# Another order of products in the last unit of each GEMM, constant matmuls ahead of the first ones, and an earlier load of the last rows

## The chip, the cores and the metric

The kernel runs on one core of a Trainium2 chip. The metric is the device time of one execution in microseconds; lower is better. The core has TensorE (PE), VectorE (DVE), ScalarE (ACT), GpSimd (POOL) and SyncE (SP), each with its own instruction stream, and 16 DMA engines. SP issues loads and stores, POOL issues transfers that add to what is in the result.

## The reference

The layer adds three things for S = 2048 rows of D = 1024: the input itself, a gated long convolution, and a feed-forward part with F = 3584.

```python
def _A_ref(q, k, v, shift_k, ssm_k, ssm_D):      # q = layernorm(x)
    k_shift = ...                                # 4-tap causal convolution of k by channel
    kv = k_shift * v
    y = irfft(rfft(kv, 2 * S) * rfft(ssm_k, 2 * S))[:S]   # causal convolution of length S
    return q * (y + kv * ssm_D)
def _B_ref(x, w1, w2):                           # x = layernorm(x)
    return silu(x @ w1) @ w2
return x + _A_ref(xn, ...) + _B_ref(xn, w1, w2)
```

Everything is in float32. Only the shapes and types of this decide the time.

## The kernel before, in words

**Products.** Every operand of a GEMM is split into a high and a low float16 part, and a product of two operands takes three matmuls (high by high, high by low, low by high) for each of four steps of 128 in the inner dimension: 12 matmuls of 512 columns. `steps` (L941, matmuls L946 to L948) does it for GEMM1, x @ w1, `steps2` (L1070, matmuls L1074 to L1076) for GEMM2, silu(...) @ w2.

**Units.** Most of GEMM1 is done by the scheme of Strassen and Winograd: a unit makes a block of two by two with seven products P1 to P7 rather than eight. `UNITS` lists 26 of them (12 for the upper half of the rows, sp = 0, then 14 for the lower half, sp = 1); four plain units with eight products stand ahead. GEMM2 begins with plain products, row tile by row tile in two halves of the columns (`TOGETHER` says which row tiles run side by side, so that they share the loaded weights), and ends with eight units of seven products (`tiles2`, L1079).

Within a unit the results are gathered partly in PSUM: P1 opens the bank `one`, ScalarE copies it into the bank `two`, then P2 is added to `one`, and P6, P5 and P3 one after another to `two`, with an eviction by ScalarE after P6 and after P5; P7 opens the bank `c`, and P4 is added to it after VectorE has read it. The order in which TensorE does them, written out in `units` (L982) and `units2` (L1092), is P7, P6, P2, P5, P1 of the next unit, P3, P4. In the last unit there is no next P1, so that P3 follows P5. `evacuate` (L909) and `evacuate2` (L1139) are the other half: what ScalarE and VectorE do with each bank. `evacuate2` scales by `invc2` and sends the four blocks of the unit to the result: three with `G` (L344), an accumulating DMA that POOL issues, and for the last unit the fourth block differently: the rows that are already in the result are loaded (`L`, L334, SP's queue), added by VectorE, and the sum is stored.

**Convolution.** It is done by a DFT as matmuls: a forward stage 1 (L1520 to L1522), products with the filter's spectrum, and an inverse (L1711 to L1713), for groups of channels `g`. They are interleaved with the GEMMs.

**Buffers.** `ff` is a ring of four PSUM banks for the products. `hfs` is a ring of three buffers with two halves each (`hf` in the trace; `vs_r` and `ws_r` are the same ring), `hts` one of two (`ht`). `places` are eight large places for factors; `XPLACE`, `W2PLACE` and `FPLACE` say what lies where and when.

**Order.** Nothing is ordered by hand beyond that. Each of the generators above is a stream, `Order.run` (L177) takes again and again the stream whose next operation can start first by a modelled clock, less a bias given to the stream:

```python
t = max(self.free[s.head.eng], s.at)
if best is None or t - s.bias < best[0]:
    best = t - s.bias, t, s
```

An operation has a modelled cost and a margin after its inputs (`T(mm, ps, [hi, lo], 0.65, m=1.0)` for TensorE). `yield ff.ready` holds a stream until a bank of the ring is free in that order, `yield made["P5"]` until another stream has issued what it names. So every edit of a cost or of a wait moves instructions of all engines elsewhere too.

**Start.** `warm_up` (L1785) issues 22 matmuls of a constant 128 by 128 tile while the first rows are loaded. Then the rows are normalized (L579), transposed by TensorE (L598), split in two by ScalarE (L360) and VectorE (L352), and the first plain unit begins.

Of the kernel before, what the change touches and what calls it, by code (L numbers as in the profile page):

```python
# [11 lines left out]
F32 = mybir.dt.float32  # L12
# [46 lines left out]
W2PLACE = [(2, 7, 6, 3, 4), (0, 1, 5, 2, 7)]  # L59
FPLACE = (6, 3, 4, 0, 1, 5, 2, 7)  # L60
# [240 lines left out]
def h3_ffn_kernel(ctx, tc, x, kp, vs, fs, shift, dskip, w1, w2, cfwd, cinv, out):  # L301
# [607 lines left out]
    def evacuate(i, b, one, c, made, seen):  # L909
# [17 lines left out]
        seen["P5"].set()  # L927
        low, done = yield from places_of(i, b + 1)
# [10 lines left out]
        add(silu(i, low, low, None, done), EB)  # L939

# [126 lines left out]
    TOGETHER = ([range(2)] + [(t,) for t in range(2, NT)],  # L1067
                [(t,) for t in range(NT - 3)] + [range(NT - 3, NT)])

    def steps2(po, hx, wc, first, last, more=False):  # L1070
        for n in range(4):
# [5 lines left out]
            yield T(mm, po, [hx[:, n], wc[:, n]], 3 * 0.2185)  # L1077
# [14 lines left out]
    def units2():  # L1092

        def product2(n, u, o, first=False):
# [4 lines left out]
            yield from steps2(o, hx, wc, first, True, not first)  # L1099
            htok.set()  # L1100
            if u == len(tiles2) - 1:
                wtok.set()

        yield ff.ready
        one = ff.tile([P, W])
        yield from product2("P1", 0, one[0], True)
        for u in range(len(tiles2)):
            made, seen = defaultdict(Token), defaultdict(Token)
            yield ff.ready
            c = ff.tile([P, W])  # L1110
            add(evacuate2(u, one, c, made, seen), EB)
            yield from product2("P7", u, c[0], True)
# [4 lines left out]
            yield from product2("P2", u, one[0])  # L1117
            made["P2"].set()
            yield seen["P6"]
            yield from product2("P5", u, two)  # L1120
            made["P5"].set()
            if u + 1 < len(tiles2):
                yield ff.ready
                one = ff.tile([P, W])
                yield from product2("P1", u + 1, one[0], True)
# [4 lines left out]
            yield from product2("P4", u, c[0])  # L1130
            made["P4"].set()
# [7 lines left out]
    def evacuate2(u, one, c, made, seen):  # L1139
# [3 lines left out]
        def copied(src, tok, to):  # L1143
            yield hfs.ready
            o, otok = hfs.tile([P, W])
# [14 lines left out]
        yield made["P2"]  # L1160
        add(copied(*one, at(u, 0, 0)), EB)
# [4 lines left out]
        seen["P5"].set()  # L1166
# [625 lines left out]
    def load_factors_late():  # L1792
        yield flag["w done"]
        yield from load_factors()
# [59 lines left out]
```

## Time and profile before

| | |
|---|---|
| median of three runs | 1255.85 us |
| the three runs | 1255.65, 1255.85, 1258.87 us |
| the profiled execution | 1258.14 us |
| its span, first to last instruction | 1256.4 us |
| mean granted clock of TensorE | 0.994 |
| TensorE busy | 1232.6 us (98%) |
| VectorE busy | 1117.9 us (89%) |
| ScalarE busy | 790.5 us (63%) |

In the profile, a row of a timeline gives the start in us, the duration, the engine, the line, the operation and its tiles (out <- in), the count, and in brackets how long the engine had been idle before and what ended that. A matmul's duration reaches to the end of its pipeline; matmuls that follow one another start closer than they last. The granted clock is 1.00 at full speed and 0.50 where the chip halves TensorE's clock.

### The profile page before, as it was taken

What the parts mean: (1) busy time and instruction counts of PE and PEld (TensorE: products, weight loads), DVE (VectorE), ACT (ScalarE), POOL (GpSimd) and SP (SyncE); (2) the same over time, 40 slices, a digit from 0 to 9 for tenths busy, and PEclk for the clock granted to TensorE, in tenths of its full rate; (3) what the DMA queues carried; (4) which work ended last, traced back from release to release, by engine and by line L of the source; (5) the groups of instructions that cost most, each with busy time, mean ns of one, the idle gap of its engine ahead of it and who ended that gap; (6) DMA issues with size and microseconds to landing.
All of it is one profiled execution on the core that took longest, in us unless ns stands there. A gap on an engine that the chain in (4) does not pass through costs nothing. (4 is left out here: it accounts for less than half of the span.)

```text
span 1256.4 us, 17146 instructions
## 1 busy us (share of the span) xinstructions
PE 1232.6 (98%) x6034; PEld 597.5 (48%) x6034; DVE 1117.9 (89%) x1359; ACT 790.5 (63%) x1431; POOL 83.5 (7%) x93
## 2 busy tenths in 40 slices
PE   7999999999999999999999999999999999999996
PEld 6554444444444544444444544544544544454452
DVE  7999987997999789998999899799989889988970
ACT  7868888886588878568654643744653545563351
POOL 0000000000000000000000000000120030123132
PEclk8999999999999999999999999999999999999999
DMA  9276989989799899769984655688595497969765
GB/s 367 82 262 239 315 288 303 300 240 227 232 336 270 242 309 313 207 191 297 311 278 125 206 179 132 185 269 231 107 257 153 106 225 217 243 137 161 164 121 80
DMA packets 272662, 279.83 MB, mean 223 GB/s; under 512 B 73792, under 2 KB 192576, under 8 KB 271296
## 3 DMA queue, kind: packets, MB, share of 16 engines
q1 hardware_dynamic: 256848, 262.22, 67.9%
q0 software_dynamic: 15728, 16.52, 9.9%
q8 instruction: 47, 0.77, 0.3%
q14 instruction: 39, 0.32, 0.1%
HBM read 175.66 MB, written 88.34 MB: 210 GB/s over the span
## 5 line engine op out<-in xcount | busy, mean ns | idle before, releaser
L1074 PE MATMUL ff<-x,wo 128*128 128x512 f16 x864 | 327.9, 380 | 3.4 <-ACT hf L360 3.4
L1076 PE MATMUL ff<-x,wo 128*128 128x512 f16 x864 | 328.1, 380 | 0.0
L1075 PE MATMUL ff<-x,wo 128*128 128x512 f16 x864 | 327.9, 380 | 0.1
L946 PE MATMUL ff<-x,wo 128*128 128x512 f16 (+1 forms) x808 | 304.5, 377 | 6.2 <-ACT hf L360 3.0
L948 PE MATMUL ff<-x,wo 128*128 128x512 f16 (+1 forms) x808 | 304.8, 377 | 1.0 <-DVE wo L352 1.0
L947 PE MATMUL ff<-x,wo 128*128 128x512 f16 (+1 forms) x808 | 304.8, 377 | 0.0
L349 DVE TENSOR_TENSOR spec<-spec 128x512 f32<-128x512 f32 (+2 forms) x256 | 261.8, 1053 | 2.0
L1075 PEld LDWEIGHTS <-wo 128*128 128x128 f16 x864 | 84.6, 98 | 104.0 <-issue 4.7
L1076 PEld LDWEIGHTS <-wo 128*128 128x128 f16 x864 | 84.6, 98 | 102.6 <-issue 1.0
L1074 PEld LDWEIGHTS <-wo 128*128 128x128 f16 x864 | 85.5, 99 | 100.1 <-issue 0.6
L948 PEld LDWEIGHTS <-wo 128*128 128x128 f16 x808 | 79.6, 98 | 94.3 <-DVE wo L352 1.5
L947 PEld LDWEIGHTS <-wo 128*128 128x128 f16 x808 | 79.5, 98 | 93.8 <-issue 5.8
L946 PEld LDWEIGHTS <-wo 128*128 128x128 f16 x808 | 81.0, 100 | 90.2 <-ACT wo L360 1.7
L349 DVE TENSOR_TENSOR tmp<-spec 128x2048 f32<-128x2048 f32 (+1 forms) x48 | 92.7, 1933 | 0.9
L352 DVE SCALAR_TENSOR_TENSOR ht<-hf,wsc,ht 128x1024 f16<-128x1024 f32 (+1 forms) x56 | 67.4, 1203 | 7.5 <-ACT ht L360 7.2
L360 ACT ACTIVATE spec<-ps 128x512 f32<-128x512 f32 x92 | 53.2, 592 | 28.7 <-PE ps L1522 28.0
L352 DVE SCALAR_TENSOR_TENSOR wo<-raw,wsc,wo 128x512 f16<-128x512 f32 (+1 forms) x56 | 56.4, 1012 | 11.9 <-ACT wo L360 11.9
L346 POOL DMA_DIRECT2D out<-hf x47 | 45.8, 981 | 303.9 <-ACT hf L360 254.4
L360 ACT ACTIVATE hf<-ff,invc 128x512 f32<-128x512 f32 x32 | 21.9, 684 | 65.7 <-PE ff L1076 47.6
L360 ACT ACTIVATE ht<-hf,wsc 128x1024 f16<-128x1024 f32 (+1 forms) x56 | 60.8, 1085 | 3.4 <-DVE hf L349 2.1
L360 ACT ACTIVATE spec<-spec 128x1024 bf16<-128x1024 f32 x32 | 33.7, 1054 | 46.1 <-DVE spec L349 46.0
L349 DVE TENSOR_TENSOR spec<-tmp 128x512 f32<-128x512 f32 (+1 forms) x80 | 61.3, 792 | 0.7
(188 smaller groups left out, 1779.3 us busy)
## 6 DMA issues: line engine op xcount, KB each, us to landing
wo<-hs SPq DMA_DIRECT2D x160, 256.0 KB, 3.2
hs<-ht SPq DMA_DIRECT2D x80, 256.0 KB, 4.8
raw<-in_w SPq DMA_DIRECT2D x28, 512.0 KB, 5.9
wraw<-in_w SPq DMA_DIRECT2D x24, 512.0 KB, 5.4
w2n<-in_w SPq DMA_DIRECT2D x24, 512.0 KB, 6.1
out<-hf POOLq DMA_DIRECT2D x47, 256.0 KB, 4.5
kin<-in_kp SPq DMA_DIRECT2D x16, 704.0 KB, 5.1
xt<-in_x SPq DMA_DIRECT2D x16, 512.0 KB, 7.3
```

What stands on the lines that cost most here:

```text
L346: return Op("POOL", 1.1, 3.0, lambda: nc.gpsimd.dma_start(o, i, accum_op=ADD), [i], [o], m, 2.3 * n)
L349: return V(lambda: nc.vector.tensor_tensor(o, a, b, op=op), o, [a, b], **k)
L352: return V(lambda: nc.vector.scalar_tensor_tensor(o, a, s, b, op0=op0, op1=op1), o, [a, b] + ([] if isinstance(s, float) else [s]), **k)
L360: nc.scalar.activation(o, i, func, scale=scale, **kw)
L946: nc.tensor.matmul(o, w[:, 0, k], xf[:, :, k, 0], start=first and k == 0, stop=False, **kw)
L947: nc.tensor.matmul(o, w[:, 0, k], xf[:, :, k, 1], start=False, stop=False, **kw)
L948: nc.tensor.matmul(o, w[:, 1, k], xf[:, :, k, 0], start=False, stop=last and k == KH - 1, **kw)
L1074: nc.tensor.matmul(po, hx[:, n, 0, :], wc[:, n, 0, :], start=first and n == 0, stop=False, **kw)
L1075: nc.tensor.matmul(po, hx[:, n, 0, :], wc[:, n, 1, :], start=False, stop=False, **kw)
L1076: nc.tensor.matmul(po, hx[:, n, 1, :], wc[:, n, 0, :], start=False, stop=last and n == 3, **kw)
```

## The change

- In the last unit of each GEMM the order of the products is P6, P7, P5, P2, P3, P4.
- `start` does P1 of a unit and begins its evacuation, which takes the bank `two`, in all units; the bank `c` is taken later, by `seventh`, just before P7.
- In the last unit of GEMM2, the rows of the result for the fourth block are loaded as soon as P6 is evicted, into a half of `hts`; copies to the result may use `hts` as well; P4 is done in two halves of 256 columns, each added and stored by itself.
- `keep_warm` issues matmuls of the constant tile, into a bank of `ff`, until the last transpose of the first rows has been issued: 23 in all, 14 of them between the second group of transposes and the first product.
- The places of some factors are exchanged, the first group of GEMM2's row tiles has three rather than two, a product's modelled cost goes with its columns, and one margin in the forward stage of the convolution is 3.0 in place of 1.0 for the first step of every group but the first.

```diff
-W2PLACE = [(2, 7, 6, 3, 4), (0, 1, 5, 2, 7)]
-FPLACE = (6, 3, 4, 0, 1, 5, 2, 7)
+W2PLACE = [(2, 6, 4, 0, 3), (1, 5, 7, 2, 6)]
+FPLACE = (4, 0, 3, 1, 5, 7, 2, 6)
 
...
         for sp in range(2):
             yield flag["room", sp]
-            yield places[4].ready
-            t, tok = places[4].tile([P, 2, 2 * W], F32)
+            r = places[(4, XPLACE["S3"])[sp]]
+            yield r.ready
+            t, tok = r.tile([P, 2, 2 * W], F32)
...
         yield made["P6"]
         yield a_act(u, two, AF.Copy)
         seen["P6"].set()
-        yield made["P2"]
-        up, both = yield from places_of(i, b)
-        add(silu(i, up[:, 0], *one, both), EB)
+
+        def first():
+            up, both = quads_up[i, b] = yield from places_of(i, b)
+            add(silu(i, up[:, 0], *one, both), EB)
+        if early:
+            yield made["P2"]
+            yield from first()
         yield ws_r.ready
         d, dt = ws_r.tile([P, 4, P])
         yield made["P5"]
         yield a_act(d, two, AF.Copy)
         seen["P5"].set()
+        c = seen["c"]
+        if not early:
+            yield made["P2"]
+            yield from first()
+        up, both = quads_up.pop((i, b))
         low, done = yield from places_of(i, b + 1)
         yield v_tt(low[:, 1], c[0], d, ADD)
...
         todo = [(i, sp) for sp in range(2) for i in UNITS[sp]]
-        yield ff.ready
-        one = ff.tile([P, 4, P])
-        yield from product("P1", *todo[0], one[0], True)
+
+        def start(n):
+            i, sp = todo[n]
+            yield ff.ready
+            one = ff.tile([P, 4, P])
+            yield from product("P1", i, sp, one[0], True)
+            made, seen = defaultdict(Token), defaultdict(Token)
+            add(evacuate(i, 2 * sp, one, made, seen, n + 1 < len(todo)), EB)
+            return one, made, seen
+
+        following = yield from start(0)
         for n, (i, sp) in enumerate(todo):
             if sp == 1:
                 flag["unit", n - len(UNITS[0])].set()
                 flag["room", 1].set()
             if i in PAIRS:
                 add(quad(i, sp), 0.1)
-            made, seen = defaultdict(Token), defaultdict(Token)
-            yield ff.ready
-            c = ff.tile([P, 4, P])
-            add(evacuate(i, 2 * sp, one, c, made, seen), EB)
-            yield from product("P7", i, sp, c[0], True)
+            one, made, seen = following
+
+            def seventh():
+                yield ff.ready
+                seen["c"] = c = ff.tile([P, 4, P])
+                yield from product("P7", i, sp, c[0], True)
+
+            def second():
+                yield from product("P2", i, sp, one[0])
+                made["P2"].set()
+            final = n + 1 == len(todo)
+            if not final:
+                yield from seventh()
             yield seen["P1"]
             two = seen["bank"][0]
             yield from product("P6", i, sp, two)
             made["P6"].set()
-            yield from product("P2", i, sp, one[0])
-            made["P2"].set()
+            yield from seventh() if final else second()
             yield seen["P6"]
             yield from product("P5", i, sp, two)
             made["P5"].set()
+            if final:
+                yield from second()
             if n + 1 < len(todo):
-                yield ff.ready
-                one = ff.tile([P, 4, P])
-                yield from product("P1", *todo[n + 1], one[0], True)
+                following = yield from start(n + 1)
             yield seen["P5"]
             yield from product("P3", i, sp, two)
             made["P3"].set()
             yield seen["P7"]
-            yield from product("P4", i, sp, c[0])
+            yield from product("P4", i, sp, seen["c"][0])
             made["P4"].set()
 
     def load_x():
         yield flag["spilled"]
-        for name in [p[0] for p in PRODUCTS.values()]:
-            r = places[XPLACE[name]]
+        for name in ("S3", "A11", "S2", "A12", "S1", "S4", "A22"):
+            r = places[4 if name == "S3" else XPLACE[name]]
             yield r.ready
...
 
 
-    TOGETHER = ([range(2)] + [(t,) for t in range(2, NT)],
+    TOGETHER = ([range(3)] + [(t,) for t in range(3, NT)],
                 [(t,) for t in range(NT - 3)] + [range(NT - 3, NT)])
...
+            yield T(mm, po, [hx[:, n], wc[:, n]], 3 * 0.2185 * size(po) / W)
...
         for u in range(len(tiles2)):
-            for n in ("P7", "P6", "P2", "P5"):
+            for n in ("P7", "P6", "P2", "P5") if u + 1 < len(tiles2) else ("P6", "P7", "P5", "P2"):
                 yield u, n
...
-        def product2(n, u, o, first=False):
+        def product2(n, u, o, first=False, cols=slice(0, W), end=True):
             yield flag["h2", u, n]
             hx, htok = flag["h2", u, n].what
             yield flag["w2f", n]
             wc, wtok = w2f[n]
-            yield from steps2(o, hx, wc, first, True, not first)
-            htok.set()
-            if u == len(tiles2) - 1:
-                wtok.set()
-
-        yield ff.ready
-        one = ff.tile([P, W])
-        yield from product2("P1", 0, one[0], True)
+            yield from steps2(o[:, cols], hx, wc[:, :, :, cols], first, True, not first)
+            if end:
+                htok.set()
+                if u == len(tiles2) - 1:
+                    wtok.set()
...
-            yield from product2("P4", u, c[0])
-            made["P4"].set()
+            if u + 1 < len(tiles2):
+                yield from product2("P4", u, seen["c"][0])
+                made["P4"].set()
+                continue
+            for q in range(2):
+                yield from product2("P4", u, seen["c"][0], cols=slice(q * W // 2, (q + 1) * W // 2), end=q == 1)
+                made["P4", q].set()
...
-    def evacuate2(u, one, c, made, seen):
+    def evacuate2(u, one, made, seen):
 
         last = u == len(tiles2) - 1
 
         def copied(src, tok, to):
-            yield hfs.ready
-            o, otok = hfs.tile([P, W])
+            yield lambda: hfs.ready() or last and hts.ready()
...
         yield made["P6"]
         yield a_act(a, two, AF.Copy, invc2[:, 0:1])
         seen["P6"].set()
-        yield made["P2"]
-        add(copied(*one, at(u, 0, 0)), EB)
+        if last:
+            yield flag["conv out"]
+            yield hts.ready
+            o, otok = hts.tile([P, W])
+            yield L(o, at(u, 1, 0))
+        if not last:
+            yield made["P2"]
+            add(copied(*one, at(u, 0, 0)), EB)
         yield ws_r.ready
         d, dt = ws_r.tile([P, W])
         yield made["P5"]
         yield a_act(d, two, AF.Copy, invc2[:, 0:1])
         seen["P5"].set()
+        c = seen["c"]
         yield v_stt(d, c[0], invc2[:, 0:1], d, MUL, ADD)
         seen["P7"].set()
+        if last:
+            yield made["P2"]
+            add(copied(*one, at(u, 0, 0)), EB)
         yield G(at(u, 1, 1), d)
         dt.set()
         if last:
-            yield flag["conv out"]
-            yield hfs.ready
-            o, otok = hfs.tile([P, W])
-            yield L(o, at(u, 1, 0))
             yield v_tt(a, a, o, ADD)
             otok.set()
         yield made["P3"]
         add(copied(two, k2, at(u, 0, 1)), EB)
-        yield made["P4"]
-        yield v_stt(a, c[0], invc2[:, 0:1], a, MUL, ADD)
+        if not last:
+            yield made["P4"]
+            yield v_stt(a, c[0], invc2[:, 0:1], a, MUL, ADD)
+            c[1].set()
+            yield G(at(u, 1, 0), a)
+            at_.set()
+            return
+        for q in range(2):
+            yield made["P4", q]
+            cols = slice(q * W // 2, (q + 1) * W // 2)
+            yield v_stt(a[:, cols], c[0][:, cols], invc2[:, 0:1], a[:, cols], MUL, ADD)
+            yield L(at(u, 1, 0)[:, cols], a[:, cols])
         c[1].set()
-        yield L(at(u, 1, 0), a) if last else G(at(u, 1, 0), a)
         at_.set()
...
+                            yield T(mm, ps, [hi, lo], 0.65, m=3.0 if g > 0 and t == TO[0] else 1.0)
                             (made if i else two[c][3]).set()
...
         tok.set()
 
+    def keep_warm():
+
+        pt, tok = ff.tile([P, 4, P])
+        while not flag["turned", "A12", 3]():
+            yield T(lambda: nc.tensor.matmul(pt[:, 0, :], ones, ones, start=True, stop=True), pt[:, 0, :], [], 0.22)
+        tok.set()
...
+    add(keep_warm(), -0.3)
     add(x_rows(), 0.13)
     add(ln_rows(), 0.03)
```

The order of the products in `uses2`, which gives the order of the loads, follows; so does the rest of `units2`, which is changed as `units` is.

More of the change, by code (lines that the diff above doesn't have):

```diff
@@ L907, in places_of, with evacuate @@
         return hf, made
-    def evacuate(i, b, one, c, made, seen):
+    def evacuate(i, b, one, made, seen, early):
         yield ff.ready
@@ L939, in evacuate @@
         add(silu(i, low, low, None, done), EB)
+    quads_up = {}
     def steps(o, w, xf, first, last, more=False):
@@ L1116, in units2 @@
             made["P6"].set()
-            yield from product2("P2", u, one[0])
-            made["P2"].set()
+            yield from seventh() if final else second()
             yield seen["P6"]
@@ L1121, in units2 @@
             made["P5"].set()
+            if final:
+                yield from second()
             if u + 1 < len(tiles2):
-                yield ff.ready
-                one = ff.tile([P, W])
-                yield from product2("P1", u + 1, one[0], True)
+                following = yield from start(u + 1)
             yield seen["P5"]
@@ L1137, in at @@
         return orr[t // T2, t % T2, :, h * W:(h + 1) * W]
-    def evacuate2(u, one, c, made, seen):
+    def evacuate2(u, one, made, seen):
         last = u == len(tiles2) - 1
         def copied(src, tok, to):
-            yield hfs.ready
-            o, otok = hfs.tile([P, W])
+            yield lambda: hfs.ready() or last and hts.ready()
+            o, otok = (hts if last and hts.ready() else hfs).tile([P, W])
             yield a_act(o, src, AF.Copy, invc2[:, 0:1])
```

26 lines of the change are left out of this document (19 added, 7 removed).

## The prediction

> **What bounds the kernel.** I read the page first, then the waits, then the timeline of each place that the waits named, and last the windows around them.
>
> ```profile
> span 1256.4 us, 17146 instructions
> PE 1232.6 (98%) x6034; PEld 597.5 (48%) x6034; DVE 1117.9 (89%) x1359; ACT 790.5 (63%) x1431; POOL 83.5 (7%) x93
> PEclk8999999999999999999999999999999999999999
> ```
>
> TensorE is busy for 98% of the span, so a kernel that does the same products can gain only where TensorE is idle, where it runs at less than full clock, or where something runs after it has ended. VectorE with 89% is the engine that could become late next. The waits of TensorE name the idle places:
>
> ```profile
> PE ff L1074 <- ACT hf L360: 3.4, 2, 2.7
> PE ff L946 <- ACT hf L360: 3.0, 1, 3.0
> ...
> PE ff L946 <- DVE hf L349: 1.8, 1, 1.8
> ```
>
> The columns are microseconds in all, times, and the longest. In the whole of GEMM1's products (L946) TensorE waited once for an eviction by ScalarE, in GEMM2's (L1074) twice; the timeline puts all three into the two last units. The windows add what the idle time costs behind it; the columns that I use are the stretch, its length, PE's busy time and, third from the end, the granted clock:
>
> ```profile
> 11.40:14.80 3.40, 1.08 (x7) 0.56 (x7) 3.23 (x12) 3.16 (x8) 0.00 (x0) 1.00 1.08 406
> 14.80:21.60 6.80, 5.83 (x28) 4.06 (x28) 6.66 (x17) 6.15 (x15) 0.00 (x0) 0.50 1.03 416
> ...
> 588.20:591.60 3.40, 3.40 (x9) 1.19 (x8) 3.37 (x4) 1.88 (x6) 0.00 (x0) 0.50 1.06 323
> ...
> 1240.20:1243.60 3.40, 3.03 (x8) 0.92 (x7) 0.00 (x0) 1.02 (x2) 0.86 (x1) 0.50 0.25 21
> ```
>
> There are three places at half clock: the first products, the last unit of GEMM1, and the last unit of GEMM2. The three edits aim at the same three places, so the working has three terms and a remainder. All are savings against the profiled execution, which took 1258.14 us for its span of 1256.4 (1.74 lie outside the span); the median of the three runs is 1255.85, 2.29 lower.
>
> **First term: the constant matmuls at the start.**
>
> ```profile
> 6.43 1.50 PE L1789 MATMUL ft<-one 128*128 128x128 f32 x12
> ...
> 12.38 0.66 PE L598 MATMUL ft<-ident,xt 128*128 128x128 f32 x4 [0.87 <-DVE x L352]
> 14.48 0.28 PE L946 MATMUL ff<-x,wo 128*128 128x256 f16 x1 [1.45 <-ACT wo L360]
> 16.07 0.40 PE L948 MATMUL ff<-x,wo 128*128 128x256 f16 x1 [0.97 <-DVE wo L352]
> 22.49 0.27 PE L948 MATMUL ff<-x,wo 128*128 128x256 f16 x1
> 22.60 1.47 PE L598 MATMUL ft<-ident,xt 128*128 128x128 f32 x12
> ...
> 20.17 0.81 DVE L579 TENSOR_SCALAR xt<-xt,ag,rstd 128x1024 f32<-128x1024 f32 x1
> 23.87 1.89 DVE L352 SCALAR_TENSOR_TENSOR x<-ft,x 128x512 f16<-128x512 f32 x3 [1.72 <-ACT x L360]
> ```
>
> The loop that warms up now (L1789, 22 instructions, each seen as two such records) gives 12 records in 1.50 us, hence 1.50 less the 0.27 that one record lasts, over 11 intervals: 0.112 each, 0.224 for one constant matmul. In the new order 14 of the 23 stand between the transposes that end at 12.38 + 0.66 = 13.04 and the first product: 14 x 0.224 = 3.1, so they end at 16.2, where the operand for L948 came at 16.07 in any case. They thus cost about 0.1 and fill the two waits of 1.45 and 0.97. If the clock then stays at 1.00, the 36 products of 256 columns ahead of the next transposes go at 0.11 each (22.49 to 22.60) and those transposes begin at 16.2 + 36 x 0.11 + 2 x 0.224 + 0.2 for the two small sums = 20.8, but not before VectorE has written their source, 20.17 + 0.81 = 20.98. Before, they began at 22.60: 1.6 earlier. What is late next is VectorE: its wait of 1.72 for the same transposes (through ScalarE) goes, and I take 1.7. Bounds: nothing, if the loads and not VectorE pace the stage that follows; 2.3, both product waits gone (1.45 + 0.97) with the constants hidden. The other nine constants lie in idle time or cost 0.2 each; that is inside the bounds.
>
> By the Trainium skill (TensorE: Matmul & The Clock Gate, "What's actually happening") the clock is granted by a window of 3.4 us that runs freely and lies otherwise in each run; the trace agrees as far as its half-clock stretches last 3.4 and twice 3.4 us, and by that rule the cold stretch here may be one window in other runs and this term nearer to its lower bound.
>
> **Second term: the last unit of GEMM1.** Before, the order P7, P6, P2, P5, P3, P4 put P3 straight behind P5, and both use the bank `two`.
>
> ```profile
> 584.66 0.38 PE L948 MATMUL ff<-x,wo 128*128 128x512 f16 x1
> 588.00 0.40 PE L946 MATMUL ff<-x,wo 128*128 128x512 f16 x1 [2.96 <-ACT hf L360]
> 591.18 0.61 PE L948 MATMUL ff<-x,wo 128*128 128x512 f16 x1
> ...
> 585.02 1.80 ACT L360 ACTIVATE py<-py,minus,csc 128x128 f32<-128x128 f32 x4
> 587.37 0.58 ACT L360 ACTIVATE hf<-ff 128x512 f32<-128x512 f32 x1
> ...
> 1244.00 0.38 PE L1074 MATMUL ff<-x,wo 128*128 128x512 f16 x1 [0.78 <-ACT hf L360]
> 1248.96 0.38 PE L1076 MATMUL ff<-x,wo 128*128 128x512 f16 x1
> ```
>
> At full clock the last 24 products of the kernel start every (1248.96 - 1244.00) / 23 = 0.216 us. So the loss here is 588.00 - 584.66 - 0.216 = 3.12 of standing still, and then 591.18 - 588.00 = 3.18 for eight intervals that take 1.73 warm, 1.45 more, and 0.2 for the ninth: 4.8. In the new order P2's 12 matmuls (12 x 0.216 = 2.6) and six matmuls of the transform (1.3) stand between P5's end and P3, 3.9 in all, against an eviction that began 587.37 - 585.04 = 2.33 after P5's end and took 0.58, 2.91 in all. The wait is covered with 1.0 to spare and the clock has no reason to fall. I take -4.3, half a microsecond less than the whole, because the transform's matmuls wait for a bank that ScalarE evicts behind this eviction. Bounds: 4.8, and 1.8 (a wait of 1.5 remains in another place with its half clock's 1.45). If the cover is gone, for which ScalarE would have to be 1 us later, each further microsecond costs one.
>
> The Trainium skill (the same page, "Why this matters for your kernels") asks for no idle gaps of TensorE above about 3 us; by that rule the gaps of 2.96 here and 2.66 at the end would cost no clock and the two terms would be less by 1.7 and 1.6. This trace shows 0.50 after both, so the measurement decides.
>
> **Third term: the last unit of GEMM2 and what runs after TensorE.**
>
> ```profile
> 1235.99 0.38 PE L1076 MATMUL ff<-x,wo 128*128 128x512 f16 x1
> 1239.03 0.38 PE L1074 MATMUL ff<-x,wo 128*128 128x512 f16 x1 [2.66 <-ACT hf L360]
> ...
> 1238.29 0.69 ACT L360 ACTIVATE hf<-ff,invc 128x512 f32<-128x512 f32 x1 [10.94 <-DMA out<-hf]
> 1249.62 0.69 ACT L360 ACTIVATE hf<-ff,invc 128x512 f32<-128x512 f32 x1 [5.67 <-DVE hf L349]
> ...
> 1230.07 1.11 POOL L346 DMA_DIRECT2D out<-ht  x1 [3.27 <-issue]
> 1234.09 1.77 POOL L346 DMA_DIRECT2D out<-hf  x2 [2.91 <-issue]
> 1250.61 0.86 POOL L346 DMA_DIRECT2D out<-hf  x1 [4.60 <-ACT hf L360]
> ...
> 1248.84 0.69 DVE L349 TENSOR_TENSOR hf<-hf 128x512 f32<-128x512 f32 x1 [4.11 <-DMA hf<-out]
> ...
> 1250.42 0.34 SPq L336 DMA_DIRECT2D out<-hf  x1
> ...
> out<-hf SPq DMA_DIRECT2D x1, 256.0 KB, 2.0
> out<-hf POOLq DMA_DIRECT2D x1, 256.0 KB, 4.1
> ```
>
> TensorE stands from 1235.99 + 0.22 to 1239.03, 2.8. From 1239.03 to 1244.00 it starts 12 products, which take 2.6 warm: 2.4 more, with the half clock and a wait of 0.78. In sum 5.2. Its cause is not ScalarE's load: ScalarE had been idle 10.94 us for an `hf` buffer which an accumulating transfer (`out<-hf`, POOL) still read. POOL's queue issues these with waits of 3.27 and 2.91 between; they wait for one another because they add to the same rows. In the new order the transfer of `d` of the unit before stands five places ahead of the last `out<-ht`, so the chain loses a link of about 3 to 4 (1230.07 to 1234.09 is 4.0), and P2 (2.6) comes between P5 and P3. What is late next is the buffer for P5's eviction: I estimate that it lands between 1.5 before P3 is due and 1.2 after, and leave 0.3 of the 5.2 in place; 4.9 gained, bounds 2.0 and 5.2.
>
> After TensorE's end (1248.96 + 0.38 = 1249.34) 7.06 us ran before. P3's copy stood until 1249.62, long after P3 was complete, because its buffer held the loaded rows until VectorE had added them, and that add at 1248.84 waited 4.11 for the load. Only then came POOL's issue at 1250.61 with 4.1 to landing (1254.7), and 1.7 to the end of the span. With the load issued as the unit begins and `ht` allowed for copies, P3's copy starts when P3 is complete, 12 x 0.216 = 2.6 before the end E of TensorE: E - 2.6 + 0.3 (an estimate of the release, from 1249.34 to VectorE's and ScalarE's next start) + 0.69 (copy) + 0.1 + 4.1 + 1.7 = E + 4.3. P4's second half: E + 0.3 + 0.45 (256 columns, an estimate from the 0.69 of 512) + 0.1 + 2.0 + 1.7 = E + 4.5. The later of the two ends the span: 7.06 - 4.5 = 2.6 gained. Bounds: 3.5, if half a store lands sooner than a whole one; 1.5, if the two half stores on SP's queue delay each other by one issue (0.34) and more. Together -7.5, between -3.5 and -8.7. No wait is put ahead of other work of POOL or SP here: the early load stands behind the last convolution row on SP's queue, and after it only stores are left.
>
> **The remainder: everything else in the order.** The scheduler is greedy and costs changed, so some hundred instructions trade places in between. TensorE's work is the same (12 products more, halves of P4). The one wait of 1.76 (below) may go or stay, another may come. I take 0, bounds -2.5 and +4.8 (one new wait like the one at 588.00).
>
> Sum: 1.7 + 4.3 + 7.5 = 13.5, so a profiled time of 1258.14 - 13.5 = 1244.6. Part of the 2.29 by which the profiled execution lies over the median may be such half-clock stretches, which the change removes in every run; then the median falls less, to 1244.6; if it is anything else, to 1255.85 - 13.5 = 1242.4. I take the middle, 1243.4, own range 1240 to 1246.5.
>
> **Rivals.** *One end keeps its wait, or the new order brings another.* For it: what releases TensorE at both ends is a chain over ScalarE, buffers and POOL, of which I could place the last link only to 1 us. Against: the order of products gives 3.9 where 2.91 are needed. It costs one such wait with its half clock, 4.8: 1248.2, range 1246.5 to 1251.5.
>
> *Slower: the bank of P7.* `start` now takes `two` for the next unit before P7 of that unit takes its bank `c`. So `c` is the bank that P3 of the unit before leaves, and P7 comes one product (P4, 2.6) behind P3, at 32 boundaries between units instead of none. It decides if the eviction of P3's bank ends later than about 2.4 after P3. Evictions that late look like this:
>
> ```profile
> 324.44 1.15 ACT L360 ACTIVATE wo<-raw,wsc 128x1024 f16<-128x1024 f32 x1 [1.23 <-PE ff L947]
> 325.49 0.67 ACT L360 ACTIVATE hf<-ff,wsc 128x512 f32<-128x512 f32 x1
> ...
> 324.23 0.38 PE L948 MATMUL ff<-x,wo 128*128 128x512 f16 x1
> 326.37 0.38 PE L946 MATMUL ff<-x,wo 128*128 128x512 f16 x1 [1.76 <-DVE hf L349]
> ```
>
> Here one operation of 1.15 stood ahead, and the bank was free at 326.16, 1.55 after the product's end at 324.61 (the wait of 1.76 was for VectorE). With two such operations ahead it is 1.15 + 1.15 + 0.67 = 2.97, 0.57 late. At all 32 boundaries that is 18.2, against the 13.5: the profiled time is then 4.7 more, the median about 1260.6. The point from which it decides is 13.5 / 32 = 0.42 a boundary. Against it: the evictions of P6 and P5 have the same room of one product now, some 60 times, and outside the last units TensorE's waits show none that was late.
>
> *No difference.* The constants do not hold the clock, and at both ends another link of the chain is late by as much as before: 1255.9.
>
> **Chances.** The forecast 0.60, the first rival 0.24, no difference 0.06, slower 0.10. About 0.3% (3.8 us) is what a measurement of this kernel can tell from no change; forecast and first rival lie beyond it: faster 0.84, same 0.06, slower 0.10. The range takes in both cases that are faster, and below them the best of all bounds, 2.3 + 4.8 + 8.7 + 2.5 = 18.3 off the median, cut to 1238.5 since not all come together: 1238.5 to 1251.5, 0.16 outside.
>
> **What would show it.** Right: clock 1.00 from the first product on and 23 more constant matmuls; no wait of L946 on ScalarE in GEMM1's last unit; a half-clock stretch in neither last unit; P3's copy within 0.5 of P3's end, and less than 5 us from TensorE's end to the span's. Wrong: a row of many small waits of P7's first matmul (L946 or L1074 on ScalarE, some 30 times), or a last unit whose wait has only moved to P7 or P2.

## The result and the profile after

The changed kernel takes 1248.48 us (median of five runs, 1247.09 to 1251.16) against 1255.85: the ratio is 0.9941, with an interval of 0.9924 to 0.9959. It is faster by 7.4 us; the forecast was 12.4. The profiled execution took 1247.09 for a span of 1245.0, 11.4 less than the span of before.

The page of the kernel after, and TensorE's waits of over 0.5 us (microseconds in all, times, longest; L958 and L1101 are the first matmuls of GEMM1's and GEMM2's products, formerly L946 and L1074):

```profile
span 1245.0 us, 17285 instructions
PE 1232.0 (99%) x6092; PEld 601.9 (48%) x6092; DVE 1118.5 (90%) x1360; ACT 788.4 (63%) x1431; POOL 83.6 (7%) x93
PEclk9999999999999999999999999999999999999999
...
PE ff L1101 <- ACT hf L360: 2.2, 1, 2.2
...
PE ff L958 <- DVE hf L349: 0.9, 1, 0.9
...
PE ff L1101 <- DVE hf L352: 0.6, 1, 0.6
```

The wait of L946 for ScalarE (3.0) is gone, and TensorE has no work at half clock in this execution (the only such stretch begins at 1244.08, after its end). A wait of 2.2 for an eviction is left in GEMM2, and one of 0.6, of a kind that was not there before, has come.

At the start, the timeline of TensorE (start, duration):

```profile
12.59 3.29 PE L1857 MATMUL ff<-one 128*128 128x128 f32 x28
20.23 1.47 PE L598 MATMUL ft<-ident,xt 128*128 128x128 f32 x12
...
45.43 0.63 PE L598 MATMUL ft<-ident,xt 128*128 128x128 f32 x4 [1.17 <-DVE x L352]
```

The 14 constant matmuls (28 records) fill the time up to the first product, and the transposes that began at 22.60 begin at 20.23. The same transposes that waited for VectorE at 47.65 before (idle 1.18) do so at 45.43, so 2.2 us are kept.

In the last unit of GEMM1, the last matmul of P5 and the first of P3, and P5's eviction by ScalarE:

```profile
580.01 0.38 PE L960 MATMUL ff<-x,wo 128*128 128x512 f16 x1
584.11 0.38 PE L958 MATMUL ff<-x,wo 128*128 128x512 f16 x1
...
581.48 0.59 ACT L360 ACTIVATE hf<-ff 128x512 f32<-128x512 f32 x1
```

The eviction is over at 582.07, 2.0 before P3, and TensorE did P2 and six matmuls of the transform in between.

In the last unit of GEMM2:

```profile
1231.95 0.38 PE L1103 MATMUL ff<-x,wo 128*128 128x512 f16 x1
1234.56 0.38 PE L1101 MATMUL ff<-x,wo 128*128 128x512 f16 x1 [2.23 <-ACT hf L360]
1239.01 0.27 PE L1103 MATMUL ff<-x,wo 128*128 128x256 f16 x1
1239.85 0.27 PE L1101 MATMUL ff<-x,wo 128*128 128x256 f16 x1 [0.57 <-DVE hf L352]
1240.40 0.27 PE L1103 MATMUL ff<-x,wo 128*128 128x256 f16 x1
...
1233.83 0.69 ACT L360 ACTIVATE hf<-ff,invc 128x512 f32<-128x512 f32 x1 [8.54 <-DMA out<-hf]
1237.35 0.69 ACT L360 ACTIVATE ht<-ff,invc 128x512 f32<-128x512 f32 x1 [2.26 <-PE ff L1103]
...
1227.61 1.78 POOL L346 DMA_DIRECT2D out<-hf  x2 [2.79 <-issue]
...
1239.32 0.48 DVE L352 SCALAR_TENSOR_TENSOR hf<-ff,invc,hf 128x256 f32<-128x256 f32 x1 [3.42 <-PE ff L1103]
1240.71 0.48 DVE L352 SCALAR_TENSOR_TENSOR hf<-ff,invc,hf 128x256 f32<-128x256 f32 x1 [0.91 <-PE ff L1103]
...
out<-hf SPq DMA_DIRECT2D x2, 128.0 KB, 3.4
out<-hf POOLq DMA_DIRECT2D x1, 256.0 KB, 4.2
...
1228.24 5.48 DMA out<-hf
```

P3 still waits: ScalarE, idle for 8.54, evicts P5 only when an accumulating transfer out of an `hf` buffer has landed, as before. Two such transfers were issued, at 1227.61 and 1228.24. The first took 4.2 (the row before the last) and so landed at 1231.8. The last row is a piece of the chain that ended last: the eviction waited for the second transfer, which landed at 1233.72, while P3 had been due since the end of P2 at 1232.33.

The 24 matmuls of 256 columns of P4 stand in TensorE's stream as 18 and 6, with VectorE's add of the first half between them. So that add begins only when the 18th has ended (1239.01 and 0.27), and the last six, which are half of the second half, wait 0.57 for it. P3's copy goes to `ht` when P3 is complete. TensorE ends at 1240.67 (the row at 1240.40, and 0.27 long), and 4.3 us run after it instead of 7.06.

### The profile page after: what moved, and what is told of

The parts are those of the page before. It is cut to its first block, busy times and chain, and to the rows that moved or that the text cites. A ratio compares the mean times of both kernels' runs of the same rounds, so it can differ in the third digit from the quotient of the medians.

```text
span 1245.0 us, 17285 instructions
## 1 busy us (share of the span) xinstructions
PE 1232.0 (99%) x6092; PEld 601.9 (48%) x6092; DVE 1118.5 (90%) x1360; ACT 788.4 (63%) x1431; POOL 83.6 (7%) x93
## 5 line engine op out<-in xcount | busy, mean ns | idle before, releaser
L1101 PE MATMUL ff<-x,wo 128*128 128x512 f16 x868 | 328.1, 378 | 2.8 <-ACT hf L360 2.2
L958 PE MATMUL ff<-x,wo 128*128 128x512 f16 (+1 forms) x808 | 302.8, 375 | 1.3 <-DVE hf L349 0.9
L1101 PEld LDWEIGHTS <-wo 128*128 128x128 f16 x868 | 85.8, 99 | 98.8
L958 PEld LDWEIGHTS <-wo 128*128 128x128 f16 x808 | 80.4, 100 | 87.9
L352 DVE SCALAR_TENSOR_TENSOR acc<-kin,taps,acc 128x1024 f32<-128x1024 f32 x48 | 61.4, 1279 | 0.6 <-ACT acc L360 0.5
L346 POOL DMA_DIRECT2D kf<-in_dskip x8 | 7.4, 922 | 801.8 <-DMA kf<-in_fs 327.2
L346 POOL DMA_DIRECT2D out<-hf x45 | 40.7, 911 | 298.5 <-ACT hf L360 201.8
```

Of the source, the lines that this page charges most:

```text
L346: return Op("POOL", 1.1, 3.0, lambda: nc.gpsimd.dma_start(o, i, accum_op=ADD), [i], [o], m, 2.3 * n)
L352: return V(lambda: nc.vector.scalar_tensor_tensor(o, a, s, b, op0=op0, op1=op1), o, [a, b] + ([] if isinstance(s, float) else [s]), **k)
L958: nc.tensor.matmul(o, w[:, 0, k], xf[:, :, k, 0], start=first and k == 0, stop=False, **kw)
L1101: nc.tensor.matmul(po, hx[:, n, 0, :], wc[:, n, 0, :], start=first and n == 0, stop=False, **kw)
```

## The experiments

All were run beside the kernel before, on three chips, with five rounds. Medians of different chips differ by up to 1.5 us, so ratios to the kernel before on the same chip are compared; one microsecond is 0.0008.

### The two kernels once more

> The kernel before, unchanged, once more. Theory 1 (the clock's windows lie otherwise in each execution): the spans of its executions differ with their mean granted clock; one with 0.994 is near the profiled 1256.4, one with 0.997 (about one half-clock stretch of 3.4 us fewer, or two) about 2 to 3.5 less, and the median lies at a clock above 0.994. Theory 2 (the profiled execution is only slower by what profiling costs): all executions show 0.994 and the spread of about 4 us has nothing to do with the clock.

> The changed kernel, unchanged, once more. Theory 1: the one wait of about 2.2 us that is left ahead of P3 in the last unit of GEMM2 is followed by a half-clock stretch in some executions and by none in others; those with a clock below 1.000 have spans 1.5 to 4 longer than those with 1.000. Theory 2: spans differ by as much among executions that all show 1.000, so the spread has another cause, such as the transfers.

Before: 1256.55 and 1255.75 (11 and 17 runs), spans from 1251.8 to 1257.2 at mean clocks from 0.992 to 0.997. Means of the span by clock: 1255.4 at 0.994 (7 runs), 1254.1 at 0.995 (9), 1252.4 at 0.997 (3). Theory 1 holds as a tendency; the correlation over the 28 is -0.74, so about half of the variance. The median span is 1254.1: the execution that I argued from, with 1256.4, lay 2.3 above it.

After: 1249.35, ratio 0.9954 (0.9940 to 0.9968). Spans at 1.000 were 1245.0 to 1246.4 and at 0.998 and 0.999 1246.8 to 1250.4 (11 runs of the two). This mean is a coarse measure, as it also counts the half clock behind TensorE's end.

The windows show what differs (the first number behind the comma is PE's busy time, the third from the end the granted clock). In each of the 14 traces the granted clock changes only at times that lie whole multiples of 3.413 us apart; in the first profile of before two stretches begin at 588.22 and 1240.17, which is 191 of them. All rows but the last of the first fence and the last of the third lie on this grid. The kernel before, second profile, with a gap of 3.35 from 1236.41 on; the kernel after, second profile, with one of 2.64 from 1232.95 on; the kernel after, first profile, with one of 2.23 from 1232.33 on:

```profile
1234.85:1238.26 3.41, 1.56 (x8) 0.59 (x6) 0.00 (x0) 0.00 (x0) 1.54 (x2) 1.00 0.72 89
1238.26:1241.67 3.41, 1.91 (x9) 0.88 (x9) 0.00 (x0) 1.15 (x2) 0.00 (x0) 1.00 0.39 65
1239.80:1243.20 3.40, 2.71 (x12) 1.13 (x12) 0.00 (x0) 1.33 (x2) 0.86 (x1) 1.00 0.03 5
```

```profile
1232.94:1236.35 3.41, 0.77 (x5) 0.38 (x4) 0.78 (x2) 1.26 (x2) 0.00 (x0) 1.00 0.30 52
1236.35:1239.77 3.42, 3.42 (x10) 1.22 (x8) 0.57 (x1) 0.00 (x0) 1.75 (x2) 0.50 0.54 65
```

```profile
1230.43:1233.84 3.41, 1.90 (x9) 0.78 (x8) 0.00 (x0) 0.01 (x1) 0.00 (x0) 1.00 0.66 106
1234.60:1238.00 3.40, 3.40 (x20) 1.90 (x20) 1.29 (x2) 1.14 (x2) 1.75 (x2) 1.00 0.32 24
```

A gap of 3.35 cost no clock, one of 2.64 did. So the length of a gap of this size does not decide; how much of it falls into one window does. The grid cuts the 3.35 into 1.85 and 1.50, the 2.64 lies whole in one window, and of the 2.23 no window holds more than 1.51. In all traces together, from the first record of the clock to TensorE's end, ten windows at full clock had 2.14 us or more of idle time, and half clock followed each; the others had 1.96 or less, and it followed none. That agrees with the free-running window of the Trainium skill that the prediction cites (TensorE: Matmul & The Clock Gate, "What's actually happening"), and its limit of about 3 us ("Why this matters for your kernels") fits neither gap. At the start the second profile of before had one half-clock stretch of 3.4 where the first had two, one behind the other; its transposes began at 21.34 instead of 22.60.

### The constants

```diff
-    add(keep_warm(), -0.3)
```

> The changed kernel without the 23 constant matmuls. Theory (they keep the clock up and cost only idle time): the first products run at half clock for one or two stretches of 3.4 us and the transposes that follow them begin 1 to 2.4 later than 20.2; the median is 1 to 2.2 above the changed kernel's 1248.5 to 1249.4, so about 1250.5. Rival (loads pace the first 50 us, so what is won at 20 us is lost again): the same median within 0.5, and the waits of the transposes near 45 us are shorter by what the start is later.

Measured 1252.85, ratio 0.9958 (0.9943 to 0.9973). The interval overlaps both of the changed kernel.

Here both pieces are put into the kernel before:

```diff
+    def keep_warm():
...
+    add(keep_warm(), -0.3)
```

> The kernel before with the constant matmuls as the only change. Theory: clock 1.00 up to the last unit of GEMM1, and 1 to 2.2 less than before: about 1254.2. The half-clock stretches of the two last units stay, so executions still differ by 2 to 4 us. Rival: the same as before within 0.5.

Measured 1254.53, ratio 0.9978 (0.9966 to 0.9990), so 2.7 less than the 1257.23 beside it (interval 1.3 to 4.3). In the changed kernel the medians put the constants' worth at between 0.5 (0.9958 against 0.9954) and 2.1 (against 0.9941); on the same chip the kernel with the old order in GEMM2, below, was 3.0 faster than the one without constants. With them the first 580 us were at full clock in each trace, without them there was a half-clock stretch in each of three. The changed kernel without constants has one, and its transposes follow it:

```profile
14.80:18.20 3.40, 2.67 (x13) 1.94 (x14) 3.40 (x8) 3.36 (x9) 0.00 (x0) 0.50 1.02 418
...
20.68 1.47 PE L598 MATMUL ft<-ident,xt 128*128 128x128 f32 x12
```

In the kernel before the theory stands. In the changed kernel the size is not settled: in this profile, the fastest of seven runs, the transposes begin 0.5 later than 20.2, not 1 to 2.4. The rival's return of the gain near 45 us was not seen: that wait is 1.17 or 1.18 in both.

### The order in the last unit of GEMM1

```diff
-            final = n + 1 == len(todo)
+            final = False
...
-            add(evacuate(i, 2 * sp, one, made, seen, n + 1 < len(todo)), EB)
+            add(evacuate(i, 2 * sp, one, made, seen, True), EB)
```

> The changed kernel with the last unit of GEMM1 in the old order P7, P6, P2, P5, P3, P4. Theory (P3 straight behind P5 waits for P5's eviction): a wait of 2.5 to 3.5 ahead of P3, with a half-clock stretch behind it in most executions: 3 to 4.8 more, a median of about 1253. Rival (the wait was ScalarE's backlog of that moment, and the new schedule has less of it): a wait of about 1, no half clock, about 1 more.

Measured 1250.51, ratio 0.9946 (0.9930 to 0.9962), within the interval of the changed kernel. The rival holds. TensorE's wait and the eviction it was for:

```profile
PE ff L958 <- ACT hf L360: 0.7, 1, 0.7
...
585.28 0.61 ACT L360 ACTIVATE hf<-ff 128x512 f32<-128x512 f32 x1
```

In the new schedule the old order has 0.70 of waiting and no half clock: P5 ended at 584.59, its eviction began 0.69 later, not 2.33 as before, and three matmuls of the transform stand ahead of P3. ScalarE has less ahead of the eviction. So most of the 4.8 that the forecast gave to the order is had without it. Which edit made ScalarE's work ahead of it less was not separated.

### The places, the loads and the margin

```diff
-W2PLACE = [(2, 6, 4, 0, 3), (1, 5, 7, 2, 6)]
-FPLACE = (4, 0, 3, 1, 5, 7, 2, 6)
+W2PLACE = [(2, 7, 6, 3, 4), (0, 1, 5, 2, 7)]
+FPLACE = (6, 3, 4, 0, 1, 5, 2, 7)
...
-    TOGETHER = ([range(3)] + [(t,) for t in range(3, NT)],
+    TOGETHER = ([range(2)] + [(t,) for t in range(2, NT)],
```

and with these the room, `load_x` and the margin of stage 1 as before.

> The changed kernel with the places of the factors, the room for the quads, the order of the x loads, the first group of GEMM2's row tiles and the margin of stage 1 as before the change; the orders of the products, the constants and the end of the last unit stay. Theory (the order covers ScalarE's backlog, as the forecast had it): the last unit of GEMM1 has no wait above 0.5 also here, and the median is within 1 of the changed kernel's. Rival (what removed that wait is the new schedule of the loads and splits, not the order): a wait of 1 to 3 comes back in the last unit of GEMM1, ahead of P3 or P4, and the median is 1.5 to 4 above.

Measured 1254.47, ratio 0.9986 (0.9974 to 0.9998): about 4 to 5.6 us of the gain are lost. The rival holds for the size. For the place it holds in part:

```profile
586.17 0.38 PE L958 MATMUL ff<-x,wo 128*128 128x512 f16 x1 [0.59 <-ACT hf L360]
590.01 0.38 PE L958 MATMUL ff<-x,wo 128*128 128x512 f16 x1 [1.09 <-DVE hf L349]
...
614.19 0.38 PE L1102 MATMUL ff<-x,wo 128*128 128x512 f16 x1 [0.49 <-DVE x L352]
617.71 0.38 PE L1102 MATMUL ff<-x,wo 128*128 128x512 f16 x1 [2.07 <-DVE x L352]
...
612.95 1.15 ACT L360 ACTIVATE x<-w2n,tau 128x1024 f16<-128x1024 f32 x1 [0.47 <-DMA w2n<-in_w]
616.38 1.28 DVE L352 SCALAR_TENSOR_TENSOR x<-w2n,tau,x 128x1024 f16<-128x1024 f32 x1
...
PE ff L1101 <- ACT hf L360: 2.8, 2, 1.4
...
1236.18 0.69 ACT L360 ACTIVATE hf<-ff,invc 128x512 f32<-128x512 f32 x1 [4.49 <-PE ff L1103]
...
q1 hardware_dynamic: 9402, 10.75, 102.0%
```

1.7 us of waiting are back around the last unit of GEMM1, and products near GEMM2's start wait 2.6 for VectorE's part of the split of w2. Its load had landed when ScalarE's part began (612.95), and VectorE, which was busy all the time from 610 to 620, came to it only at 616.38. The DMA engines were full from 590 to 620 (the last row: packets, MB, share of 16 engines), but so they were in the changed kernel (103.1%), which has no such wait. The kernel before had none either; it came to GEMM2 at 597.46, after its 4.8 of waiting, this one at 592.60. So without the new places a gain at the end of GEMM1 seems to be given back in part at the start of GEMM2. Later two more waits for evictions come, 2.8 in all, and the one that the changed kernel has in the last unit is gone: P5's eviction, the row at 1236.18, waits for TensorE and not for a transfer.

All its runs were at clocks of 0.998 to 1.000, with spans from 1248.7 to 1257.2, and the profile is of the fastest. These waits tell of that execution alone, and what makes the others up to 8.5 longer no trace shows. Which of the edits of this group does it was not separated.

### The end of GEMM2: order, buffer, halves, load

```diff
-            final = u + 1 == len(tiles2)
+            final = False
...
-            for n in ("P7", "P6", "P2", "P5") if u + 1 < len(tiles2) else ("P6", "P7", "P5", "P2"):
+            for n in ("P7", "P6", "P2", "P5"):
```

> The changed kernel with the last unit of GEMM2 in the old order; the early load, the ht buffers for copies and the halves of P4 stay. Theory (the buffer chain, not the order, sets this end): P5 waits for the eviction of P6 or P3 for that of P5 until the transfers of the unit before have landed, as in the changed kernel 2.2 to 2.7 in all, and 0.8 more for P3 straight behind P5: a median 0.5 to 1.5 above the changed kernel. Rival (the order itself removes the wait that the kernel before had): a wait of about 2.7 plus 0.8 and a half-clock stretch each time, 2.5 to 4 more.

Measured 1249.88, ratio 0.9937 (0.9921 to 0.9953): no difference from the changed kernel that can be told. One wait, as long as there, with a half-clock stretch behind it (from 1237.45 on) as in that kernel's second profile:

```profile
PE ff L1101 <- ACT hf L360: 2.5, 1, 2.5
```

In both orders four products of the last unit stand ahead of P3, so that it is due at the same point, and the buffer sets when it begins. The theory holds; its further 0.8 did not appear.

```diff
-        yield ws_r.ready
-        d, dt = ws_r.tile([P, W])
+        yield (hts if last else ws_r).ready
+        d, dt = (hts if last else ws_r).tile([P, W])
```

> The changed kernel with the evicted P5 of the last unit in a half of the ht buffers instead of hf. Theory of the buffer (the wait of 2.23 ahead of P3 is for an hf half that an accumulating transfer still reads): P5's eviction starts within 0.4 of P5's end, the wait ahead of P3 is gone, TensorE ends 2.2 earlier and the span is about 2 shorter than that of the changed kernel, with the clock at 1.000 in every execution: median about 1246. Rival (the chain of accumulating transfers sets the end, not TensorE): TensorE ends 2.2 earlier but P3's copy or its transfer waits for the transfers ahead, and the span is less than 0.7 shorter.

Measured 1245.79, ratio 0.9918 (0.9905 to 0.9930), 3.6 us below the changed kernel beside it (1249.35, 0.9954), and the intervals are apart. Clocks were 0.999 and 1.000. P5's eviction by ScalarE, and the only wait that GEMM2's products have left:

```profile
1231.68 0.69 ACT L360 ACTIVATE ht<-ff,invc 128x512 f32<-128x512 f32 x1 [4.49 <-PE ff L1103]
...
1239.36 0.27 PE L1101 MATMUL ff<-x,wo 128*128 128x256 f16 x1 [0.58 <-DVE hf L352]
```

ScalarE now waits for TensorE and not for a transfer. That the buffer was the cause is shown.

With the buffer mended, the two old orders again (edits as above):

> The changed kernel with P5's eviction of the last unit in ht, and both last units in the old order of products. Theory (each eviction costs 0.7 to 0.9 where nothing stands between P5 and P3, if neither buffer nor backlog delays it): 0.7 of waiting in each of the two last units, no half-clock stretch, a median 1.4 above that with P5 in ht and the new orders, about 1247.2. Rival (the order alone carries the gain): waits of 2 to 3 with half clocks in both, 5 or more above.

Measured 1248.22, ratio 0.9934 (0.9923 to 0.9946), 2.0 above the 0.9918 of the new orders (in ratios). Waits of 0.71 and 0.78 ahead of P3, and no work at half clock in the trace: the theory holds. So the order is worth about 1.5 to 2 once nothing else is late; the intervals overlap by a little.

```diff
...
-            for q in range(2):
-                yield from product2("P4", u, seen["c"][0], cols=slice(q * W // 2, (q + 1) * W // 2), end=q == 1)
-                made["P4", q].set()
+            yield from product2("P4", u, seen["c"][0])
+            made["P4"].set()
```

and one add and one store.

> The changed kernel with P4 of the last unit in one piece, as before the change: one add of 512 columns and one store of 256 KB. Theory of the shared bank (the second half's matmuls wait until VectorE has read the first half, the 0.57 of idle time): the wait goes, TensorE ends 0.57 earlier, the add takes 0.75 instead of 0.48 and the end of the span is the same within 0.5. Rival (the forecast's step: halves bring the end nearer by half an add and a smaller store): the span is 0.6 to 1.2 longer than with halves.

Measured 1249.29, ratio 0.9948 (0.9936 to 0.9960): the halves make no difference that can be told. The wait of 0.57 is gone with them. The shared bank alone does not make that wait: in the kernel with the late load, the last of these runs, the scheduler put both adds behind all of P4, the bank is the same, and the wait does not appear.

```diff
-                yield from product2("P7", u, c[0], True)
+                if not final:
+                    yield from product2("P7", u, c[0], True)
+                    return
+                yield ff.ready
+                seen["c2"] = c2 = ff.tile([P, W])
+                for q in range(2):
+                    h = (c, c2)[q][0]
+                    yield from product2("P7", u, h, True, cols=slice(q * W // 2, (q + 1) * W // 2), end=q == 1)
```

with P4's second half, its add and that of `d` taken from `c2`, and `d` in `ht`.

> The changed kernel with P5's eviction in ht, and the halves of P7 and P4 of the last unit in two banks. Theory (the 0.57 of idle time is the shared bank): TensorE ends 0.57 earlier than with P5 in ht alone, the last add follows 0.3 behind it, and the span is 0.4 to 0.7 shorter: a median of about 1245.3. Rival (the transfer of P3's copy over POOL's queue lands last): TensorE ends earlier but the span stays within 0.2.

Measured 1245.16, ratio 0.9911 (0.9898 to 0.9924). This is the fastest of all; against 0.9918 the step is 0.9, and the intervals overlap. TensorE's longest wait behind the first 50 us is now

```profile
PE ff L958 <- DVE hf L349: 0.9, 1, 0.9
```

and none is left in the two last units.

```diff
-        if last:
-            yield flag["conv out"]
-            ...
-            yield L(o, at(u, 1, 0))
...
         if last:
+            yield flag["conv out"]
+            ...
+            yield L(o, at(u, 1, 0))
             yield v_tt(a, a, o, ADD)
```

> The changed kernel with the load of the last rows issued where it was before, behind the eviction of P5 and its add; copies may still use ht. Theory (the load of about 2 to 4 us is hidden by P2, P3 and P4 in either place, because ht takes the copies): the load lands 1 to 3 before P4's first half is complete, and the span is the same within 0.5. Rival (the early load is what shortened the tail): VectorE's add waits for it until after P4's first half, and the tail behind TensorE is 1 to 2.5 longer.

Measured 1249.06, ratio 0.9941 (0.9929 to 0.9953): the earlier issue of the load is worth nothing that can be told. The scheduler issued it at 1223.16 instead of 1217.29, and VectorE added the rows at 1235.25, when P5's eviction let it. P3's copy began at 1237.39, as it did at 1237.35 with the early load. What shortened the tail is then most likely `ht`, which holds the loaded rows and the copies; a kernel without `ht` for one or the other was not run.

## Why the prediction was right and wrong

The time lies in the stated range, the sign was right, and what happened is of the kind of the first rival: one end keeps its wait. That rival was worked out at 1248.2; 1248.48 was measured. So close a match is in part luck: the rival priced the wait with its half clock at 4.8, and the profile after keeps 2.8 and no half clock. The forecast itself was wrong by 5.1: 2.5 in the profiled time (1247.09 against 1244.6), and 2.6 in the step from the profile to the median, which was put at -1.2 and was +1.4.

**Start, forecast 1.7: right, in part by luck.** 2.2 in the first pair of profiles, 0.6 in the second (46.38 against 45.76 for the transposes that wait for VectorE), 2.7 between medians with this edit alone. The two half-clock stretches that I priced are one in other executions (the second profile, 21.34 against 22.60).

**End of GEMM1, forecast 4.3 by the order: the size was right, the cause was not.** The wait of 2.96 and the half clock behind it, 4.8, are gone in every trace of the changed kernel. But with the old order 0.70 of waiting remains of it, and the median is no worse than could be told. The step that failed was to cost the order of products against ScalarE's old backlog, as if the rest of the schedule stayed.

**End of GEMM2, forecast 4.9 in TensorE: the step that failed.** I left 0.3 of 5.2 and estimated P5's buffer to be free between 1.5 before P3 is due and 1.2 after. It came free 1.4 after (1233.72 against 1232.33), and 1.8 in the second profile. The last link was the step: P5's eviction had been given the buffer of the second of two transfers, and that of the first came free 1.9 earlier, before P3 was due. The 0.3 is also about what that estimate gives for the buffer alone (1.2 x 1.2 / 2 / 2.7 = 0.27, if all times between are equally likely), without the 0.7 of the eviction. So P3 was 2.2 and 2.6 late. With the end of P4, whose wait for VectorE's add I had not named at all, 2.8 of 5.0 remained in the first profile (2.66 + 0.78 + 1.6 of half clock before, 2.23 + 0.57 after), and in the second the half clock behind the gap as well. Another buffer for P5 takes the wait away and brings 3.6.

**Tail, forecast 2.6: right in size (2.7) in the first pair of profiles, partly wrong in its reason.** In the second pair it is 5.0 (8.6 against 3.6). The earlier issue of the load does nothing that can be told; P3's copy, no longer held by the loaded rows, begins as P3 is complete. The half stores did not land sooner than the whole: 3.9 and 2.8 against 2.0.

**The remainder, forecast 0: the sum was right, the reason wrong.** The waits between the ends add up to about as much as before. But I gave the edits of places and loads no term, and without them 4 to 5.6 of the 7.4 are lost. The trace without them suggests that they pay in part for what the earlier end of GEMM1 makes late; it covers only the fastest execution.

**The slower rival did not happen.** No row of small waits of P7's first matmul at the boundaries appears: TensorE waits once on L1101 for ScalarE, in the last unit, and on L958 never by 0.5 or more for an eviction by ScalarE.

**From the profile to the median.** The sum of the four terms for the profiled pair is 2.2 + 4.8 + 2.2 + 2.7 = 11.9, and its spans differ by 11.4. Between the medians it is 7.4: the profiled span of before lay 2.3 above the median of 28, that of after 2.0 below the median of its 11 (1247.0). Taking the middle between the two readings of the 2.29 was not enough, since the wait that was left also brings its half clock only in some executions. The time outside the span also rose from 1.74 to 2.09.

## What to carry to other kernels

When one wait is taken away, ask who releases the engine that releases it: here ScalarE was idle, and a buffer that a transfer still read set the time in both orders. A stage that ends earlier may need its successor's operands earlier; edits that move loads belong in the sum even where no wait is seen at them. And executions of one kernel may differ by most of the change (5.4 us of span for either kernel here, against 7.4), so compare the spans and granted clocks of many runs before a term is sized from one.

## What the runs showed of the hardware

The granted clock changed only on a grid of 3.413 us, which lay otherwise in each execution. TensorE's idle time within one window of the grid decided: 2.14 to 2.96 of it were followed by half clock (ten windows), 1.96 or less were not. So gaps of 2.23, 3.09 (GEMM2's last unit in the kernel with GEMM1's old order) and 3.35 that the grid cut in two cost no clock, and one of 2.64 that it left whole did. Ahead of TensorE's end a stretch lasted 3.4 us, but for the one of 6.8 at the start of the first profile of before: there the first window at half clock had 0.97 of idle time itself, where 0.74 or less was followed by full clock.

Two stores of 128 KB, issued 1.4 apart, took 3.9 and 2.8 us to land in the first profile of after (3.1 and 2.1 in the second); one of 256 KB took 2.0 in the kernel before and 2.5 in the changed one with P4 whole. So a store of half the size did not land sooner here.
